# Loads of two chunks split over two queues, in longer runs, and a new order for the opening

## The chip, the cores and the metric

The kernel runs on one core of one Trainium2 chip. The metric is the device time of one execution in microseconds, lower is better. TensorE (PE) does the matrix products and the transposes into PSUM, VectorE (DVE), ScalarE (ACT) and GpSimd (POOL) do the elementwise work, and SyncE (SP) issues most of the transfers. Each engine works through its own list of instructions in the order in which they stand, and waits on semaphores for what other engines or transfers must have done.

## The reference

Attention over 4 batches, 8 heads, 768 tokens and head size 64, where a token sees the first 4 tokens (the sinks) and the last 128. Its output, seen as 3072 rows of 512, goes through a feed-forward layer that takes the largest of three products:

```python
scores = scale * np.matmul(q, k.transpose(0, 1, 3, 2))
is_sink = pos[None, :] < int(n_sink)
in_window = (rel >= 0) & (rel < int(window))
scores = np.where(is_sink | in_window, scores, -1000000000.0)
a = np.exp(scores - np.max(scores, axis=-1, keepdims=True))
a = a / (np.sum(a, axis=-1, keepdims=True) + 1e-09)
attn = np.matmul(a, v)
x = attn.transpose(0, 2, 1, 3).reshape(B * S, H * D)
h = np.maximum(np.maximum(x @ w1, x @ w2), x @ w3)      # 512 -> 768
out = h @ w_out                                         # 768 -> 512
```

All arrays are float32; the kernel computes in bf16 with float32 sums.

## The kernel before, in words

The 3072 rows are cut into 12 chunks of 256 tokens, three to a batch. The 8 heads are handled as 4 pairs. A chunk goes through these steps:

- `load` (L76 to L93): K, Q and V of the chunk, 512 KB each, from SyncE's queue. Partition p holds tokens 2p and 2p+1 of all heads, so a contiguous run is 2 tokens of one head, 512 bytes. A `gate` is a tiny POOL instruction that writes into the target first; the load waits for it, and so starts only when POOL has come that far (`pool_gate`, a memset) or when a weight has landed (`after`).
- `cast_qk` (L95) and `cast_v` (L104): float32 to bf16, in halves of four heads (`g` is 0 or 1) or quarters, each on an engine that the order names.
- `turn2` (L129, chunks 0 and 1) and `turn` (L109, chunks 2 and 3): four transposes on TensorE for a half, and one copy out of PSUM (the evacuation, L144 for K, L141 for Q), on the engine that the order names. With `turn2` K and Q of one half share a PSUM bank. From chunk 4 on, `turn_dma` does this by a transfer.
- `premask` (L251) puts the additive mask into PSUM with two matmuls on a pair ahead of its scores; pairs without it get a multiplicative mask after the exponential (`mask`, L289, on VectorE).
- `score` (L259), `expo` (L282, ScalarE), for chunks 1 and 2 of a batch also `sink_score` (L294); `sink_k` and `sink_v` (L226, L310) cut out the sinks' keys and values, `sink_init` (L216) prepares them.
- `av_open` and `av` (L324, L339): the product with V for a pair, then on VectorE a reciprocal (L355) and a product (L358) that normalise it.
- `xpose` (L364): eight transposes of the chunk's attention output, two evacuations.
- `ffn_h` (L383): a block of 8 matmuls (L390) for one third of the 768 columns and one of the three weights; ScalarE copies the first weight's result (L397), VectorE takes the largest with the other two (L401). `ffn_y` (L406) is the last product, `store` writes it.

PSUM has 8 banks, handed out in turn by `bank` and `give`. The weights come by GpSimd's queue (`load_w`, L236, in pieces of columns; `load_wo`, L244), which casts them on the way.

For chunks 0 to 3 the order is written out by hand, call by call (L454 to L655): it sets the order of the instructions on every engine and queue. `warm(n)` puts n idle matmuls into TensorE's list. After that a loop (L656) treats every chunk alike.

What the change touches: `load`, `cast_qk`, `turn2`, the first exponential (L168, which loads ScalarE's table) and the list from L454 on.

Of the kernel before, what the change touches and what calls it, by code (L numbers as in the profile page):

```python
# [16 lines left out]
def kernel(  # L17
# [13 lines left out]
    nc = tc.nc  # L31
# [17 lines left out]
    with tc.manual_schedule():  # L49
# [26 lines left out]
        def load(ci, what="kqv", gate=None, part=None, parts=1):  # L76
# [4 lines left out]
            for w in what:  # L81
# [13 lines left out]
        def cast_qk(ci, w, g, eng):  # L95

            if (ci, w) not in bfs:
                bfs[ci, w] = raw.tile([128, NP, 2, 2, D], BF16, tag=w + "_bf", name=w + "_bf")
            x, y = bfs[ci, w], raws[ci, w]
            f = eng.copy if eng is nc.scalar else eng.tensor_copy  # L100
            f(x[:, 2 * g:2 * g + 2].rearrange("q p i a d -> q p a i d"),  # L101
              y[:, 4 * g:4 * g + 4].rearrange("q (p a) i d -> q p a i d", a=2))
# [26 lines left out]
        def turn2(ci, w, g, eng=None):  # L129
# [10 lines left out]
            if w == "q":  # L140
                f(  # L141
                    qT[ci % RING][:, 2 * g:2 * g + 2].rearrange("q p i n r -> q (p i) (n r)"), pt)
            else:
                f(  # L144
                    kT[ci % RING][:, :, 2 * g:2 * g + 2].rearrange("q n p i r -> q n (p i) r"),
                    pt.rearrange("q x (n r) -> q n x r", r=64))
# [21 lines left out]
        nc.scalar.activation(one, wz[:, 0:1], AF.Exp)  # L168
        for x in vb:
            nc.vector.memset(x[:, :, :, D:D + 1], 1.0)  # L170

# [282 lines left out]
        warm(6)  # L454
        load(0, 'k')
        load(0, 'q', gate=pool_gate)
        warm(6)
        masks()
        premask(0, (2,))
        load(0, 'v', gate=pool_gate)  # L460
        cast_qk(0, 'k', 0, nc.gpsimd)
        sink_init()
        cast_qk(0, 'k', 1, nc.vector)
        premask(0, (3,))
        cast_qk(0, 'q', 0, nc.scalar)
        cast_qk(0, 'q', 1, nc.vector)
        turn2(0, 'k', 0, nc.scalar)
        load(1, 'k')
        premask(0, (0,))
        turn2(0, 'k', 1, nc.scalar)  # L470
        turn2(0, 'q', 1, nc.scalar)
        turn2(0, 'q', 0, nc.vector)
        score(0, (0,))
        expo(0, 0)
        load(1, 'q')
        premask(0, (1,))
        sink_k(0)
        cast_v(0, 1, 1, nc.vector)
        load_w(0, 0, 768)
        score(0, (1,))  # L480
        score(0, (2,))
        warm(3)
        cast_qk(1, 'k', 0, nc.vector)
        cast_v(0, 0, 0, nc.vector)
        cast_v(0, 1, 0, nc.gpsimd)
        expo(0, 2)
        expo(0, 1)
        load(1, 'v')
        av_open(0)
        load_w(1, 512, 768)  # L490
        score(0, (3,))
        cast_v(0, 0, 1, nc.vector)
        cast_qk(1, 'q', 1, nc.gpsimd)
        cast_qk(1, 'k', 1, nc.vector)
        av(0, 0)
        expo(0, 3)
        cast_qk(1, 'q', 0, nc.vector)
        turn2(1, 'k', 0, nc.vector)
        load_w(1, 0, 512)
        cast_v(1, 0, 1, nc.gpsimd)  # L500
        sink_v(0)
        av(0, 1)
        turn2(1, 'k', 1, nc.scalar)
        turn2(1, 'q', 0, nc.vector)
        turn2(1, 'q', 1, nc.vector)
        av(0, 2)
# [3 lines left out]
        av(0, 3)  # L510
        load_w(2, 0, 256)
        score(1, (0,))
        cast_v(1, 1, 1, nc.vector)
        score(1, (2,))
        premask(1, (3,))
        load_w(2, 256, 512)
        load(2, 'q', gate=pool_gate)
        score(1, (3,))
        load_w(2, 512, 768)
        expo(1, 0)  # L520
        xpose(0, 0, nc.vector)
        cast_qk(2, 'k', 1, nc.gpsimd)
        xpose(0, 1, nc.vector)
        expo(1, 2)
        sink_score(1)
        expo(1, 3)
        premask(1, (1,))
        load(2, 'v', gate=after(1))
        mask(1, 0)
        load_wo()  # L530
        cast_v(1, 1, 0, nc.vector)
        av_open(1)
        score(1, (1,))
        mask(1, 2)
        load(3, 'q', gate=after(0))
        ffn_h(0, 0, 0)
        cast_v(2, 1, 0, nc.gpsimd)
        expo(1, 1)
        av(1, 0)
        av(1, 2)  # L540
        ffn_h(0, 1, 0)
        av(1, 3)
        ffn_h(0, 2, 0)
        av(1, 1)
        ffn_h(0, 2, 1)
        xpose(1, 0, nc.scalar)
        xpose(1, 1, nc.vector)
        ffn_h(0, 0, 1)
        ffn_h(1, 0, 0)
        ffn_h(0, 1, 1)  # L550
        cast_qk(2, 'q', 0, nc.vector)
        ffn_h(1, 1, 0)
        ffn_h(1, 1, 1)
        cast_qk(2, 'k', 0, nc.scalar)
        cast_qk(2, 'q', 1, nc.scalar)
        turn(2, 'k', 1, nc.scalar)
        ffn_h(1, 2, 0)
        load(3, 'k', gate=after(1))
        turn(2, 'k', 0, nc.vector)
        ffn_h(1, 2, 1)  # L560
        ffn_h(1, 0, 1)
        turn(2, 'q', 0, nc.scalar)
        turn(2, 'q', 1, nc.scalar)
        ffn_h(0, 0, 2)
        score(2, (0,))
        score(2, (1,))
        ffn_h(1, 1, 2)
        expo(2, 0)
        ffn_h(0, 1, 2)
        score(2, (3,))  # L570
        expo(2, 1)
        cast_v(2, 0, 1, nc.vector)
        mask(2, 0)
        load(4, 'q', gate=pool_gate)
        score(2, (2,))
        load(3, 'v', gate=after(2))
        sink_score(2)
        mask(2, 1)
        ffn_h(0, 2, 2)
        ffn_h(1, 0, 2)  # L580
        expo(2, 3)
        cast_v(2, 1, 1, nc.gpsimd)
        expo(2, 2)
        cast_qk(3, 'q', 1, nc.vector)
        ffn_y(0, 0)
        load(4, 'k', gate=after(2))
        cast_v(2, 0, 0, nc.gpsimd)
        mask(2, 2)
        av_open(2)
        av(2, 0)  # L590
        cast_qk(3, 'q', 0, nc.gpsimd)
        cast_qk(3, 'k', 1, nc.scalar)
        mask(2, 3)
        av(2, 1)
        cast_qk(3, 'k', 0, nc.gpsimd)
        turn(3, 'q', 1, nc.vector)
        ffn_h(1, 2, 2)
# [152 lines left out]
```

## Time and profile before

| | |
|---|---|
| median of 3 runs | 179.97 us (179.81 to 180.43) |
| profiled execution | 180.04 us, its span 178.3 us |
| TensorE's granted clock | 1.000 |
| busy: PE, DVE, ACT, POOL | 170.4, 129.2, 81.4, 64.6 us |
| first warm-up matmul, first score, first FFN matmul (L390) | 1.20, 9.62, 18.33 us |
| Q of chunk 0: issued, cast begins | 1.38, 6.72 us |
| loads of 512 KB by SyncE, median from issue to landing | K 5.0, Q 6.1, V 7.1 us |

The span runs from the first to the last instruction of the profiled execution; the time of a run lies 1.7 us above it. In lines of the timeline the first number is the start in us, the second the busy time, then engine, line, operation, output and input, shapes and count; in brackets stands the idle time before it and what ended it. In lines of groups the numbers behind the bar are busy us, mean ns of one, and idle time of the engine before them. A line of a stretch gives the stretch, its length, the busy us of PE, PE's weight loads, DVE, ACT and POOL with counts, the granted clock, the transfer engines' busy share and GB/s.

### The profile page before, as it was taken

What the parts mean: (1) busy time and instruction counts of PE and PEld (TensorE: products, weight loads), DVE (VectorE), ACT (ScalarE), POOL (GpSimd) and SP (SyncE); (2) the same over time, 40 slices, a digit from 0 to 9 for tenths busy, and PEclk for the clock granted to TensorE, in tenths of its full rate; (3) what the DMA queues carried; (4) which work ended last, traced back from release to release, by engine and by line L of the source; (5) the groups of instructions that cost most, each with busy time, mean ns of one, the idle gap of its engine ahead of it and who ended that gap; (6) DMA issues with size and microseconds to landing.
All of it is one profiled execution on the core that took longest, in us unless ns stands there. A gap on an engine that the chain in (4) does not pass through costs nothing.

```text
span 178.3 us, 4662 instructions
## 1 busy us (share of the span) xinstructions
PE 170.4 (96%) x1873; PEld 126.3 (71%) x1873; DVE 129.2 (72%) x277; ACT 81.4 (46%) x163; POOL 64.6 (36%) x121
## 2 busy tenths in 40 slices
PE   7689999999999999999999999999999999999991
PEld 2445889766687587587696696696795795796870
DVE  3189752799799796696794994994975975976451
ACT  3386734863962922912715715615426426420210
POOL 4478620323663793282280670670550000000000
PEclk9999999999999999999999999999999999999999
DMA  5999999999999997995996996996978707202203
GB/s 147 290 286 209 243 212 249 214 288 290 332 184 258 295 170 184 256 279 129 293 282 136 299 210 152 296 215 155 285 211 136 162 0 64 119 6 56 118 0 118
DMA packets 69029, 34.90 MB, mean 196 GB/s; under 512 B 26512, under 2 KB 67472, under 8 KB 69008
## 3 DMA queue, kind: packets, MB, share of 16 engines
q1 hardware_dynamic: 64912, 31.33, 78.1%
q0 software_dynamic: 3952, 3.15, 11.3%
q8 instruction: 14, 0.23, 0.5%
q10 hardware_dynamic: 144, 0.13, 0.2%
q14 instruction: 7, 0.06, 0.1%
HBM read 25.17 MB, written 6.29 MB: 176 GB/s over the span
## 4 chain that ended last, share of the span: by engine, by line
PE 79%; DMA 13%; POOL 2%; ACT 2%; issue 1%; DVE 1%; POOLq 0%; ACTq 0%
PE h_ps L390 47%; PE y_ps L411 18%; DMA q_raw<-in_q_dram 9%; PE o L350 6%; PE st L274 5%; DMA w<-in_moe_w_dram 5%; PE o L332 1%; POOL w L239 1%; PE y_ps L421 1%; ACT q_bf L101 1%; PE sk L300 1%; PE xt L371 1%; ACT kT L144 1%; PE pt L115 1%; DVE h_sb L401 0%
## 5 line engine op out<-in xcount | busy, mean ns | idle before, releaser
L390 PE MATMUL h_ps<-xT,w 128*128 128x256 bf16 x864 | 103.8, 273 | 0.2 <-DVE h_sb L401 0.2
L390 PEld LDWEIGHTS <-w 128*128 128x128 bf16 x864 | 81.3, 98 | 11.7 <-issue 0.6
L401 DVE TENSOR_TENSOR h_sb<-h_sb,h_ps 128x512 bf16<-128x512 bf16 (+1 forms) x74 | 49.1, 669 | 17.5 <-PE h_ps L390 14.9
L397 ACT CAST h_sb<-h_ps 128x512 bf16<-128x512 f32 x36 | 21.1, 587 | 59.5 <-PE h_ps L390 59.4
L286 ACT ACTIVATE e_sb<-st 128x512 bf16<-128x512 f32 (+1 forms) x96 | 45.7, 573 | 5.1 <-PE st L274 5.0
L411 PE MATMUL y_ps<-wo,h_sb 128*128 128x512 bf16 x138 | 33.6, 380 | 0.0
L105 POOL CAST vb<-v_raw 64x512 bf16<-64x512 f32 x40 | 25.9, 648 | 19.8 <-DMA v_raw<-in_v_dram 18.2
L292 DVE TENSOR_TENSOR e_sb<-e_sb,msk 128x1024 bf16<-128x1024 bf16 (+1 forms) x42 | 30.0, 748 | 1.1 <-ACT e_sb L286 1.0
L101 POOL CAST k_bf<-k_raw 128x512 bf16<-128x512 f32 x17 | 12.8, 772 | 41.4 <-DMA k_raw<-in_k_dram 39.9
L413 DVE COPY y_sb<-y_ps 128x512 f32<-128x512 f32 x19 | 13.1, 691 | 13.0 <-PE y_ps L411 12.7
L411 PEld LDWEIGHTS <-h_sb 128*128 128x128 bf16 x138 | 11.9, 98 | 14.0 <-issue 2.5
L358 DVE TENSOR_TENSOR x_sb<-o,rc 128x256 bf16<-128x256 f32 x48 | 20.4, 424 | 1.7
L350 PE MATMUL o<-vb,e_sb 128*128 128x65 bf16 x352 | 18.3, 194 | 0.3 <-DVE vb L105 0.2
L350 PEld LDWEIGHTS <-e_sb 128*128 128x128 bf16 x352 | 16.0, 98 | 2.6 <-DVE vb L105 0.4
L274 PE MATMUL st<-qT,kT 64*128 64x128 bf16 (+1 forms) x256 | 14.3, 238 | 0.6 <-DVE qT L141 0.6
L274 PEld LDWEIGHTS <-kT 64*128 64x128 bf16 x256 | 8.2, 94 | 7.9 <-issue 6.2
L101 POOL CAST q_bf<-q_raw 128x512 bf16<-128x512 f32 x17 | 12.3, 742 | 4.1 <-DMA q_raw<-in_q_dram 3.7
L355 DVE RECIPROCAL rc<-o 128x4 f32<-128x4 f32 x48 | 8.4, 175 | 1.2 <-PE o L350 0.9
L306 ACT ACTIVATE e_sink<-sk 128x256 bf16<-128x256 f32 x8 | 3.1, 384 | 8.9 <-PE sk L300 8.9
L177 PE MATMUL warm<-wz 128*128 128x512 bf16 x15 | 5.2, 507 | 1.2 <-DVE wz L166 1.2
L101 DVE CAST q_bf<-q_raw 128x512 bf16<-128x512 f32 x5 | 2.1, 422 | 4.5 <-DMA q_raw<-in_q_dram 4.5
L239 POOL DMA_DIRECT2D w<-in_moe_w_dram x6 | 4.9, 810 | 0.1
(70 smaller groups left out, 69.8 us busy)
## 6 DMA issues: line engine op xcount, KB each, us to landing
k_raw<-in_k_dram SPq DMA_DIRECT2D x12, 512.0 KB, 5.0
q_raw<-in_q_dram SPq DMA_DIRECT2D x12, 512.0 KB, 6.1
v_raw<-in_v_dram SPq DMA_DIRECT2D x12, 512.0 KB, 7.1
out_dram<-y_sb SPq DMA_DIRECT2D x11, 512.0 KB, 3.7
w<-in_moe_w_dram POOLq DMA_DIRECT2D x4, 256.0 KB, 9.1
w<-in_moe_w_dram POOLq DMA_DIRECT2D x1, 768.0 KB, 8.3
wo<-in_moe_w_out_dram POOLq DMA_DIRECT2D x1, 768.0 KB, 10.7
w<-in_moe_w_dram POOLq DMA_DIRECT2D x1, 512.0 KB, 9.4
```

The source lines that it names most:

```text
L101: f(x[:, 2 * g:2 * g + 2].rearrange("q p i a d -> q p a i d"), y[:, 4 * g:4 * g + 4].rearrange("q (p a) i d -> q p a i d", a=2))
L105: eng.tensor_copy(vb[ci % RING][64 * i:64 * i + 64, n, :, 0:D], raws[ci, "v"][64 * n:64 * n + 64, :, i])
L274: nc.tensor.matmul(st[a][:, s:s + q1 - q0].rearrange("q n (i r) -> q n i r", i=2), lhsT=x[hp, n, p].rearrange("q i r -> q (i r)"), rhs=qc[ ...
L286: nc.scalar.activation(e[:, a, lo:], st[a][:, lo:], AF.Exp, scale=scale)
L292: (eng or nc.vector).tensor_mul(e[:, :, lo:], e[:, :, lo:], msk0 if lo else msk)
L350: nc.tensor.matmul(o[:, t, a], lhsT=e[:, a, s], rhs=vb[cv % RING][:, n, 2 * p + a], start=first, stop=True, skip_group_check=True)
L358: nc.vector.tensor_mul(xs[ci][:, :, p], o[:, :, :, 0:D], rc.unsqueeze(3).to_broadcast([128, 2, 2, D]))
L390: nc.tensor.matmul(hp[:, f].rearrange("q (i t r) -> q i t r", i=2, t=2), lhsT=w_sb[wi][:, ds, c0:c0 + 128], rhs=xTs[ci][:, :, ds].rearrang ...
L397: nc.scalar.copy(dst, hp)
L401: nc.vector.tensor_max(dst[:, x], dst[:, x], hp[:, x])
L411: nc.tensor.matmul(yp, lhsT=hs[ci][:, fb, t * 128:(t + 1) * 128], rhs=wo[:, fb], start=(fb == 0), stop=(fb == FB - 1))
L413: (nc.scalar.copy if eng is None else eng.tensor_copy)(ys[ci][:, t], yp)
```

## The change

The loads of chunks 0 and 1 are each cut into two, one issued by SyncE and one by ScalarE, without gates. For V each half holds four heads. For K and Q each half holds four heads on 64 partitions, and a partition holds four tokens of a head in one run of 1024 bytes. So the upper and the lower 64 partitions belong to different heads, and a token's place inside a transposed block is another: `cast_qk` regroups the heads, and the evacuations of `turn2` put the tokens back in order. They read PSUM with two neighbouring outputs 256 elements apart. K's evacuation becomes two copies of 256 elements in place of one of 512; a half `g` now covers pairs g and g+2.

The first exponential moves behind the first loads on ScalarE. The list for chunks 0 to 3 is ordered anew: which engine does a cast or an evacuation, the masks first, 16 warm-up matmuls in place of 15, one pair of chunk 1 with an additive mask in place of two, other gates and places for the loads of chunks 2 to 5 (Q of chunk 2 in two parts), other places for blocks of `ffn_h`. The loop is the same.

```diff
@@ load
+                if ci < 2:
+                    for g, e in enumerate((nc.sync, nc.scalar)):
+                        if w == "v":
+                            e.dma_start(
+                                out=dst[:, 4 * g:4 * g + 4],
+                                in_=src[b, 4 * g:4 * g + 4, t0:t0 + 256]
+                                    .rearrange("h (p i) d -> p h (i d)", i=2))
+                        else:
+                            e.dma_start(
+                                out=dst[64 * g:64 * g + 64].rearrange("r h i d -> r (h i d)")
+                                    .rearrange("r (h e) -> r h e", h=4),
+                                in_=src[b, 4 * g:4 * g + 4, t0:t0 + 256]
+                                    .rearrange("h (r j) d -> r h (j d)", j=4))
+                    continue
@@ cast_qk
+            if ci < 2:
+                n = H // 2
+                f(x[:, 2 * g:2 * g + 2].rearrange("q p i a d -> q (p i) a d")
+                  .rearrange("q j a d -> q a j d"),
+                  y[:, n * g:n * g + n].rearrange("q h i d -> q (h i d)")
+                  .rearrange("q (a j d) -> q a j d", a=2, d=D))
+                return
@@ turn2
             if w == "q":
-                f(
-                    qT[ci % RING][:, 2 * g:2 * g + 2].rearrange("q p i n r -> q (p i) (n r)"), pt)
+                f(qT[ci % RING][:, g:NP:2].rearrange("q h i n r -> q h i (n r)")
+                  .rearrange("q h i (m j) -> q h i m j", j=2),
+                  pt.rearrange("q (j i) (h m) -> q h i m j", i=2, h=2))
             else:
-                f(
-                    kT[ci % RING][:, :, 2 * g:2 * g + 2].rearrange("q n p i r -> q n (p i) r"),
-                    pt.rearrange("q x (n r) -> q n x r", r=64))
+                y = pt.rearrange("q x (h n m) -> q x h n m", h=2, n=2)
+                for n in range(2):
+                    f(kT[ci % RING][:, n, g:NP:2].rearrange("q h i (m j) -> q h i m j", j=2),
+                      y[:, :, :, n].rearrange("q (j i) h m -> q h i m j", i=2))
@@ the order, chunks 0 and 1 (after)
+        masks()
+        load(0, 'k')
+        load(0, 'q')
+        warm(9)
+        table()
+        load(0, 'v')
+        load(1, 'k')
+        cast_qk(0, 'k', 0, nc.gpsimd)
+        premask(0, (0,))
+        load(1, 'q')
+        load(1, 'v')
+        warm(2)
+        cast_qk(0, 'k', 1, nc.gpsimd)
+        cast_qk(0, 'q', 1, nc.vector)
+        turn2(0, 'k', 1, nc.vector)
+        cast_qk(0, 'q', 0, nc.scalar)
+        turn2(0, 'k', 0, nc.scalar)
+        turn2(0, 'q', 1, nc.scalar)
+        premask(0, (3,))
+        premask(0, (1,))
+        sink_init()
+        sink_k(0)
+        turn2(0, 'q', 0, nc.vector)
+        score(0, (0,))
...
+        warm(5)
...
+        load(2, 'q', part=0, parts=2, gate=pool_gate)
...
+        load(2, 'q', part=1, parts=2)
...
+        load(2, 'v')
...
+        ffn_h(1, 0, 0)
+        turn(2, 'q', 0, nc.scalar)
+        turn(2, 'k', 0, nc.vector)
...
```

More of the change, by code (lines that the diff above doesn't have):

```diff
@@ L472 @@
+        turn2(0, 'q', 1, nc.scalar)
+        premask(0, (3,))
+        premask(0, (1,))
+        sink_init()
+        sink_k(0)
         turn2(0, 'q', 0, nc.vector)
         score(0, (0,))
+        premask(0, (2,))
+        load_w(0, 0, 768)
+        score(0, (3,))
         expo(0, 0)
[L475 to L479, printed above, removed]
[L480 to L483 removed]
@@ L528 @@
[L528 to L536, printed above, removed]
+        expo(1, 0)
+        load(2, 'q', part=0, parts=2, gate=pool_gate)
+        score(1, (3,))
+        score(1, (1,))
+        load_w(2, 256, 512)
+        xpose(0, 0, nc.vector)
+        cast_v(1, 1, 1, nc.vector)
+        expo(1, 1)
+        load_w(2, 512, 768)
@@ L563 @@
-        turn(2, 'q', 1, nc.scalar)
-        ffn_h(0, 0, 2)
+        load(3, 'v', gate=pool_gate)
+        ffn_h(1, 1, 2)
+        expo(2, 1)
+        load(4, 'q', gate=after(0, 300))
+        ffn_h(0, 1, 2)
         score(2, (0,))
-        score(2, (1,))
-        ffn_h(1, 1, 2)
         expo(2, 0)
-        ffn_h(0, 1, 2)
+        mask(2, 1)
+        mask(2, 0)
         score(2, (3,))
[L571 to L574, printed above, removed]
+        cast_v(2, 0, 1, nc.gpsimd)
@@ L627 @@
         mask(3, 1)
-        score(3, (3,))
         mask(3, 0)
         expo(3, 2)
-        turn_dma(4, 'k')
-        cast_v(4, 0, 1, nc.gpsimd)
+        load(5, 'v', gate=after(2))
+        ffn_h(2, 0, 1)
         ffn_h(2, 0, 2)
         expo(3, 3)
-        cast_v(3, 1, 0, nc.gpsimd)
-        cast_v(4, 1, 1, nc.vector)
-        ffn_h(2, 0, 1)
+        av_open(3)
+        cast_v(4, 1, 1, nc.gpsimd)
+        mask(3, 2)
+        mask(3, 3)
         ffn_h(2, 2, 0)
-        mask(3, 3)
+        av(3, 0)
```

185 lines of the change are left out of this document (85 added, 100 removed).

## The prediction

> **What bounds the kernel now.** I read the page's shares first, then busy time by stretches, then the timeline of the opening, then mean durations by shape, and last the chain that ended last.
>
> ```profile
> PE 170.4 (96%) x1873; PEld 126.3 (71%) x1873; DVE 129.2 (72%) x277; ACT 81.4 (46%) x163; POOL 64.6 (36%) x121
> PE   7689999999999999999999999999999999999991
> ```
>
> PE is the bound. Only the first three slices (13 us) and the last one fall short, so the change can win only in the opening; what it does to the order of chunks 2 to 4 can hardly win, but it can lose. By stretches (busy us of each engine, granted clock, DMA share, GB/s):
>
> ```profile
> 2.00:4.00 2.00, 2.00 (x6) 0.73 (x5) 1.08 (x6) 0.23 (x2) 0.86 (x4) 1.00 0.89 245
> 4.00:6.00 2.00, 2.00 (x10) 0.93 (x9) 0.43 (x1) 0.00 (x0) 0.91 (x3) 1.00 1.21 298
> 6.00:8.00 2.00, 0.99 (x12) 0.72 (x10) 0.43 (x1) 1.22 (x3) 0.55 (x4) 1.00 1.21 290
> 8.00:10.00 2.00, 0.99 (x13) 0.75 (x13) 0.83 (x2) 0.98 (x3) 1.29 (x3) 1.00 1.21 291
> 14.00:16.00 2.00, 1.98 (x34) 1.26 (x31) 1.90 (x8) 0.84 (x3) 1.83 (x3) 1.00 1.17 213
> 16.00:18.00 2.00, 2.00 (x29) 0.97 (x28) 1.91 (x5) 2.00 (x5) 1.75 (x4) 1.00 1.32 202
> 45.50:46.00 0.50, 0.50 (x4) 0.19 (x2) 0.50 (x2) 0.50 (x2) 0.50 (x1) 1.00 1.10 395
> ```
>
> PE idles 2 us between 6 and 10, while the loads run at 290 GB/s. From 14 us PE is full; but VectorE is busy 1.90 of each 2 us there, so a longer VectorE operation in that stretch is not free.
>
> ```profile
> 1.38 5.31 DMA q_raw<-in_q_dram
> 20.14 10.03 DMA q_raw<-in_q_dram
> ```
>
> In the chain, Q of chunk 0 lands at 6.69. I count the opening from that instant.
>
> ```profile
> 6.72 0.43 DVE L101 CAST q_bf<-q_raw 128x512 bf16<-128x512 f32 x1 [1.38 <-DMA q_raw<-in_q_dram]
> 6.78 0.62 ACT L101 CAST q_bf<-q_raw 128x512 bf16<-128x512 f32 x1 [4.54 <-DMA q_raw<-in_q_dram]
> 7.30 1.07 ACT L144 COPY kT<-pt 128x512 bf16<-128x512 bf16 x2
> 8.42 0.61 PE L137 MATMUL pt<-ident,q_bf 128*128 128x128 bf16 x8 [1.43 <-ACT kT L144]
> 9.14 0.42 DVE L141 COPY qT<-pt 128x512 bf16<-128x512 bf16 x1 [1.99 <-PE pt L137]
> 9.62 0.34 PE L274 MATMUL st<-qT,kT 64*128 64x256 bf16 x4 [0.59 <-DVE qT L141]
> 9.97 3.29 ACT L286 ACTIVATE e_sb<-st 128x384 bf16<-128x384 f32 x8 [0.55 <-PE st L274]
> ```
>
> Q cast, both K evacuations on ScalarE, Q transposes, Q evacuation, first score: 2.93 us after the landing. The first FFN matmuls (L390) start at 18.33, which is 11.64 after the landing, and from there PE hardly waits. So the question is when the new kernel has done the same work. Durations by shape:
>
> ```profile
> L141 DVE COPY qT<-pt 128x512 bf16<-128x512 bf16 x3 | 1.2, 419 | 2.0 <-PE pt L137 2.0
> L423 DVE COPY y_sb<-y_ps 128x256 f32<-128x256 f32 x1 | 0.4, 425 | 0.6 <-PE y_ps L421 0.6
> L413 DVE COPY y_sb<-y_ps 128x512 f32<-128x512 f32 x19 | 13.1, 691 | 13.0 <-PE y_ps L411 12.7
> L144 ACT COPY kT<-pt 128x512 bf16<-128x512 bf16 x3 | 1.7, 585 | 0.3 <-PE pt L137 0.3
> L423 ACT COPY y_sb<-y_ps 128x256 f32<-128x256 f32 x1 | 0.4, 372 | 3.1 <-PE y_ps L421 3.1
> ```
>
> **The change, part by part.**
>
> *The loads.* K and Q of chunk 0 are 1.05 MB; summing the stretches they have moved by 5.85, and Q lands 0.85 later. With runs of 1 KB and two queues the rate is not in the trace. Best end: 395 GB/s (the stretch at 45.5, with runs of 4 KB) from 2.0 on, 2.66 us, landing at 5.5. Worst end: 220 GB/s, what the stretches from 24 to 28 show while two queues share the engines: 4.8 us, landing at 7.6. Between: the slow first microsecond (144 KB from 2 to 3) carries twice the bytes, then 350 to 395 GB/s, landing at 5.8 to 6.05. I take 5.9, since the nearest rows are those of whole loads without a rival; 0.8 earlier than now.
> [...]
>
> *ScalarE's six issues.* An issue takes 0.37 to 0.45 (the rows on SP and the one on ScalarE). Two go ahead of the table load, which ends near 3.2 instead of 2.2: hidden, ScalarE has nothing to do before Q lands. In the changed program's order the fifth and sixth issue of each queue wait for the K half and the Q half of chunk 0. On ScalarE the Q cast stands behind them, so it starts 0.35 after the landing. Ends: 0, if that half lands early; 1.7, if an issue is held as SP's fourth to sixth are now (1.38 and 1.74 each). I take 0.35: only half as many bytes stand in each queue.
>
> *Casts.* Same shapes (0.43 DVE, 0.62 ACT, 0.61 to 0.78 POOL). Both K casts of chunk 0 now run on POOL one after the other, done 1.5 after K lands (about 4.4), so by 5.9: hidden behind Q.
>
> *Evacuations.* The new layout reads PSUM with neighbours 256 elements apart, K in two copies of 256. No row shows such a read. On VectorE the rows go by words fetched: 512 neighbouring bf16 are 256 words, 0.42; 256 f32 words 0.425; 512 words 0.69. Ends: 0.29 for each K copy and 0.42 for Q if it still fetches pairs (the 128x130 copy took 0.29), 0.425 and 0.69 if each element is a fetch. I take the latter, as no two neighbours share a word: K 0.85 for 0.42, Q 0.69 for 0.42. ScalarE takes 0.59 for 512 of either type, so only K's split counts: 0.74 for 0.59.
> [...]
>
> *From Q's landing to the first score.* VectorE: cast 0.46, K evacuation 0.85 (now beside ScalarE, not behind its Q cast); PE: transposes 0.25, two masks' matmuls (L256) 0.65, transposes and hand-over 0.45; VectorE: Q evacuation 0.69. Sum 3.40 with the hand-overs (2.93 now); 2.9 with the cheap copies. ScalarE's own path (0.35+0.62+0.74) ends earlier, at 1.75.
>
> *From there to the first FFN matmul.* The fifth exponential frees the bank for sink_v: 0.35+5x0.41=2.40. Then VectorE's order is one chain: sink_v and hand-over 0.45, its copy 0.28, casts of K and Q of chunk 1 0.43 each, K evacuation 0.85, reciprocal and product of two pairs 1.2, Q evacuation 0.69, two pairs more 1.2. Then PE: eight transposes, sink scores, one pair's mask, one score, 1.4. Sum 9.33. The 16 warm-up matmuls (15 now), POOL's K cast of chunk 1 (ready near 11.7, when the chain needs it), its weight issues and the chunk-1 loads (landing before 12.1 even at today's rate) all lie beside that chain. On POOL the masks come first and sink_init after the K casts; sink_k follows the K evacuation, so w1's load is issued near 8.3 (9.08 now) and lands before 17.3, ahead of L390; were it late, PE would wait there by as much.
>
> *Sum.* 5.9+3.4+9.3=18.6; the sink part of chunk 1 (0.25), which now stands ahead of L390's first block, comes after it, so 18.9 against 18.33: +0.55. The pair-mask matmul saved in chunk 1 and the extra mask product (0.69 on VectorE, beside PE's FFN) are in it. The profiled execution took 180.04, 0.07 above the median of 179.97; against the median I forecast 180.5.
>
> *Chunks 2 to 4.* PE's idle time in the stretches from 14 to 60 sums to about 0.4, so at most that is won; I put the reorder at 0. Q of chunk 2 goes in two parts, one issue more on SP (0.37), which has nothing behind it but later loads; what could be late is its landing (third rival).
>
> **Rivals.**
> 1. *Faster: the strided evacuations cost what they cost now.* It is decided on VectorE between 6 and 16 us: two K evacuations at 0.58 and two of Q at 0.42 take 1.08 out of the sum, giving 17.8, -0.5; with the loads at 5.6, -0.8: 179.2. It is level with now when the four save 0.55 together. For it: 0.42 and 0.29 are rows of bf16 copies; against: the word count.
> 2. *Slower: the loads come no sooner.* Landing 6.7 with the strided copies: +1.35, 181.3. For it: DMA share is 1.2 already; against: 395 GB/s with long runs.
> 3. *Slower: Q of chunk 2 is late.* Its transposes move three FFN blocks forward (0.87 each), to about 27.5. Issued near 18.9, with today's 10.03 us it lands at 28.9, and cast and PE follow at 29.4: +1.9, 182.3. Against: 2 us of the opening's loads are gone by then, and it goes ahead of V; the row is of a time when w2 and wo ran beside it.
> 4. *Faster: the reorder removes waits.* -0.4 for all idle time that PE has there, and -0.8 if VectorE's chain runs without the hand-overs that I count between PE and VectorE: 179.3. For it: VectorE loses a K cast, a V cast and two evacuations to POOL and ScalarE in this stretch; against: what it loses is not on the chain.
>
> **How the numbers follow.** Forecast 0.45 (own range 180.1 to 181.1), rival 1 0.22, rival 2 0.13, rival 3 0.10, rival 4 0.10. 0.3% (0.54 us) is what a measurement of this kernel can tell from no change. The forecast lies on that edge: 0.21 of its chance is within, 0.24 above. Faster 0.31 (rivals 1 and 4, less 0.01), same 0.22, slower 0.47. Range 179.0 to 182.2: it takes in rivals 1, 2 and 4 and the loads' bounds for the most part, and leaves out the end of rival 3 and best loads with cheap copies.
>
> **What would show it.** Q of chunk 0 landing near 5.9, ScalarE's cast 0.35 behind VectorE's; VectorE's kT copies at 0.42 each and qT at 0.69; first score near 9.3; L390 from about 18.6 with PE waiting near 13 (K evacuation) and 16.5 (x of the last pair). Wrong if the copies take 0.3 and 0.42, if the landing is under 5.3, or if PE stalls at L390 or the chunk-2 transposes between 26 and 30.

## The result and the profile after

The changed kernel takes 185.42 us (median of 4 runs, 183.88 to 186.44), the kernel before 180.01 on the same chip: 1.028 times as long, 95% interval [1.0237, 1.0317]. Ratios here and below compare runs in the chip's faster state; medians and ranges hold all runs. Forecast were 180.5, and a range up to 182.2. The profiled execution of after is the run of 183.88, with a span of 182.1; that of before took 180.04, with a span of 178.3. So the traces show 3.84 us of the loss. The three other runs took 185.09 to 186.44, at mean granted clocks of 0.981 down to 0.972, where the profiled one has 0.990. If all that is missing is time at 0.50, the clock of the stretch from 12 to 14 us below, the profiled run spent about 3.5 us at it and the others 7 to 10 (an estimate from these means); that would account for most of the 1.5 us between the profiled run and the median, but there is no trace of those runs.

The page's busy shares and slices, after:

```profile
PE 170.6 (94%) x1859; PEld 126.9 (70%) x1872; DVE 129.6 (71%) x279; ACT 81.8 (45%) x166; POOL 62.5 (34%) x119
...
PE   7368899999999999999999999999999999999991
...
PEclk9978999999999999999999999999999999999999
```

TensorE is busy for as long as before (170.6 against 170.4 us) in a span that is 3.8 longer: the loss is mostly idle time, and it stands in the first four slices. There the granted clock also falls below full speed, which it did not before. By stretches (columns as before: busy us of PE, PE's weight loads, DVE, ACT, POOL; granted clock, DMA share, GB/s), after:

```profile
2.00:4.00 2.00, 2.00 (x6) 0.76 (x5) 1.08 (x6) 1.49 (x2) 0.73 (x3) 1.00 0.88 193
4.00:6.00 2.00, 1.69 (x7) 0.54 (x5) 0.00 (x0) 0.00 (x0) 0.00 (x0) 1.00 1.14 222
6.00:8.00 2.00, 0.62 (x8) 0.45 (x8) 0.00 (x0) 0.00 (x0) 1.83 (x7) 1.00 1.18 211
8.00:10.00 2.00, 0.37 (x5) 0.41 (x6) 1.09 (x3) 1.16 (x3) 0.18 (x2) 1.00 1.18 269
10.00:12.00 2.00, 1.15 (x13) 0.72 (x10) 0.98 (x2) 0.58 (x1) 1.71 (x5) 0.83 1.15 239
12.00:14.00 2.00, 2.00 (x18) 0.79 (x15) 0.92 (x2) 1.41 (x4) 1.96 (x5) 0.50 1.14 256
```

From 4 to 8 us the loads move 222 and 211 GB/s, where before moved 298 and 290, at a DMA share of 1.14 and 1.18 (1.21 before): the transfer engines are nearly as full as before and deliver a quarter less. (The share adds up the times of all packets, so it can pass 1.) From 6 to 10 us TensorE works 0.62 and 0.37 of each 2 us, and behind that comes the clock of 0.50.

The chain that ended last names the landing of chunk 0's Q (start, us, what):

```profile
1.54 6.84 DMA q_raw<-in_q_dram
```

It lands at 8.38, where before had 6.69. The timeline of the opening, after, from the cast of chunk 0's Q to the first FFN matmul (start us, us; the bracket is idle time and what ended it):

```profile
8.49 0.43 DVE L117 CAST q_bf<-q_raw 128x512 bf16<-128x512 f32 x1 [4.75 <-DMA q_raw<-in_q_dram]
8.82 0.62 ACT L117 CAST q_bf<-q_raw 128x512 bf16<-128x512 f32 x1 [5.18 <-DMA q_raw<-in_q_dram]
8.83 0.75 DVE L168 COPY kT<-pt 128x256 bf16<-128x256 bf16 x2
...
10.99 0.69 DVE L162 COPY qT<-pt 128x512 bf16<-128x512 bf16 x1 [1.42 <-PE pt L158]
11.74 0.51 PE L299 MATMUL st<-qT,kT 64*128 64x256 bf16 x4 [0.85 <-DVE qT L162]
12.93 1.14 PE L299 MATMUL st<-qT,kT 64*128 64x256 bf16 x12
...
21.89 1.05 PE L415 MATMUL h_ps<-xT,w 128*128 128x256 bf16 x8
```

VectorE's cast of Q starts at 8.49 (6.72 before), the first score at 11.74 (9.62 before), the first FFN matmul at 21.89 (18.33 before): 3.56 of the 3.84 us are lost by then.

### The profile page after: what moved, and what is told of

It is laid out like the page before. It is cut to its first block, busy times and chain, and to the rows that moved or that the text cites. A ratio compares the mean times of both kernels' runs of the same rounds, so it can differ in the third digit from the quotient of the medians.

```text
span 182.1 us, 4661 instructions
## 1 busy us (share of the span) xinstructions
PE 170.6 (94%) x1859; PEld 126.9 (70%) x1872; DVE 129.6 (71%) x279; ACT 81.8 (45%) x166; POOL 62.5 (34%) x119
## 4 chain that ended last, share of the span: by engine, by line
PE 86%; DVE 6%; DMA 4%; issue 2%; SPq 0%; DVEq 0%
PE h_ps L415 50%; PE y_ps L436 17%; PE st L299 6%; PE o L375 6%; DMA q_raw<-in_q_dram 4%; DVE h_sb L426 1%; PE o L357 1%; PE st L281 1%; PE pt L136 1%; DVE x_sb L383 1%; PE xt L396 1%; DVE qT L162 1%; PE warm L202 1%; DVE kT L168 1%; PE sk L325 1%
## 5 line engine op out<-in xcount | busy, mean ns | idle before, releaser
L436 PE MATMUL y_ps<-wo,h_sb 128*128 128x512 bf16 x126 | 32.7, 380 | 0.6
L122 POOL CAST k_bf<-k_raw 128x512 bf16<-128x512 f32 x16 | 10.9, 701 | 37.6 <-DMA k_raw<-in_k_dram 37.5
L375 PE MATMUL o<-vb,e_sb 128*128 128x65 bf16 x352 | 17.4, 193 | 0.0
L375 PEld LDWEIGHTS <-e_sb 128*128 128x128 bf16 x352 | 15.4, 98 | 1.6
L299 PE MATMUL st<-qT,kT 64*128 64x128 bf16 (+1 forms) x256 | 14.9, 245 | 1.4 <-DVE qT L162 1.1
L299 PEld LDWEIGHTS <-kT 64*128 64x128 bf16 x256 | 8.7, 96 | 8.4 <-issue 6.6
L122 POOL CAST q_bf<-q_raw 128x512 bf16<-128x512 f32 x14 | 10.2, 752 | 3.9 <-DMA q_raw<-in_q_dram 3.8
L202 PE MATMUL warm<-wz 128*128 128x512 bf16 x15 | 5.7, 523 | 1.4 <-DVE wz L189 1.2
L202 PEld LDWEIGHTS <-wz 128*128 128x128 bf16 x16 | 1.9, 127 | 4.2 <-issue 2.7
```

The source lines that it names most:

```text
L299: nc.tensor.matmul(st[a][:, s:s + q1 - q0].rearrange("q n (i r) -> q n i r", i=2), lhsT=x[hp, n, p].rearrange("q i r -> q (i r)"), rhs=qc[ ...
L375: nc.tensor.matmul(o[:, t, a], lhsT=e[:, a, s], rhs=vb[cv % RING][:, n, 2 * p + a], start=first, stop=True, skip_group_check=True)
L436: nc.tensor.matmul(yp, lhsT=hs[ci][:, fb, t * 128:(t + 1) * 128], rhs=wo[:, fb], start=(fb == 0), stop=(fb == FB - 1))
```

## The experiments

First the loads, then the clock, then the order, then the loads in the old order. In each diff the lines with a minus are those of the kernel that the text names.

**Two queues, but every transfer over all partitions.** The changed kernel, with K and Q of chunks 0 and 1 in halves by heads, like V; layout, casts and copies as before.

```diff
-                        if w == "v":
+                        if True:     # halves of 4 heads on 128 partitions
...
```

> The changed kernel, but K and Q of chunks 0 and 1 go as V does: each half is four heads on all 128 partitions in runs of two tokens, by both queues; casts and evacuations are the old ones. Theory R (rows: a half that writes only 64 partitions fills half of the memory's side and runs near 215 GB/s): the halves are whole again in partitions, so Q of chunk 0 lands near 6.7 as before the change; with the cheap evacuations the first FFN matmul follows 12.0 to 12.4 later, near 18.9, time near 181. Theory S (two queues at once slow each other, whatever the shape): Q still lands at 8.0 or later, first FFN matmul past 20, time 183 or more. Theory L (the long runs are slow): as theory R.

Measured: 181.44 (before beside it 180.19), ratio 1.0072 [1.0046, 1.0097]. Stretches of this run:

```profile
4.00:6.00 2.00, 2.00 (x7) 0.78 (x6) 0.00 (x0) 0.00 (x0) 1.26 (x3) 1.00 1.20 302
6.00:8.00 2.00, 1.15 (x15) 0.92 (x14) 0.76 (x2) 0.19 (x1) 0.59 (x4) 1.00 1.21 290
```

Two queues give the rate of one (298 and 290 before), and VectorE's Q cast starts at 6.83: two queues by themselves neither won nor lost bandwidth here. What this kernel loses in the opening shows on ScalarE:

```profile
6.83 0.37 ACTq L89 DMA_DIRECT2D q_raw<-in_q_dram  x1
6.83 0.43 DVE L115 CAST q_bf<-q_raw 128x512 bf16<-128x512 f32 x1 [3.10 <-DMA q_raw<-in_q_dram]
7.24 0.52 ACTq L89 DMA_DIRECT2D v_raw<-in_v_dram  x1
7.81 0.62 ACT L115 CAST q_bf<-q_raw 128x512 bf16<-128x512 f32 x1 [4.42 <-DMA q_raw<-in_q_dram]
```

The issues of chunk 1's Q and V stand ahead of ScalarE's cast and go out only when Q of chunk 0 lands, so the cast starts 0.98 behind VectorE's. The first score comes at 9.94 and the first FFN matmul at 19.21, where the order alone (below) has 9.46 and 18.41.

**One queue, but halves on 64 partitions.**

```diff
-                    for g, e in enumerate((nc.sync, nc.scalar)):
+                    for g, e in enumerate((nc.sync, nc.sync)):
```

> The changed kernel with both halves issued by SyncE, one after the other; layout, casts and evacuations as changed. Theory R (rows): still 215 GB/s, 1.05 MB take 4.9 us from 2 on, Q lands at 7.8 or later, time 183 or more. Theory S (two queues): one queue runs near 290 GB/s, Q lands by 6.9, first FFN matmul near 20, time near 182. Theory L (long runs): as R.

Measured: 185.49, ratio 1.0278 [1.0227, 1.0329], the same as the changed kernel. Its stretches:

```profile
4.00:6.00 2.00, 2.00 (x7) 0.70 (x5) 0.00 (x0) 0.00 (x0) 0.07 (x1) 1.00 1.14 209
6.00:8.00 2.00, 0.87 (x10) 0.45 (x8) 0.00 (x0) 0.00 (x0) 1.78 (x7) 1.00 1.19 215
```

Without a second queue the rate is as low: it belongs to the transfers on 64 partitions. From 4 to 6 us only K and Q move, here and in the changed kernel, and a packet of 1 KB takes 88 and 83 ns. From 6 to 8 about half of the bytes are V's. Its halves go over all partitions and are slow there too: a packet of 512 bytes takes 49 ns in the changed kernel, 34 in the kernel before. Why V suffers no run shows.

**Halves on every other partition.** Two queues and runs of 1 KB as in the changed kernel, but a half takes partitions g, g+2, and so on; the copies out of PSUM take the heads from the last index instead of the first.

```diff
-                                out=dst[64 * g:64 * g + 64].rearrange("r h i d -> r (h i d)")
+                                out=dst[g:128:2].rearrange("r h i d -> r (h i d)")
...
-                  pt.rearrange("q (j i) (h m) -> q h i m j", i=2, h=2))
+                  pt.rearrange("q (j i) (m h) -> q h i m j", i=2, h=2))
...
```

> The changed kernel with the halves on every other partition (even rows the first four heads, odd rows the others) in place of the lower and upper 64; two queues and runs of four tokens as changed, the same number of casts and evacuations. Theory R (rows): each half reaches all of the memory's side, Q lands between 5.5 and 6.5, the first FFN matmul 13.0 to 13.4 later, near 19.2, time near 181. Theories S and L: Q lands past 8, time 183.5 to 185.5 as changed.

Measured: 183.31 (181.46 to 184.38), ratio 1.0143 [1.0081, 1.0204]. The stretch that answers to the 222 of the changed kernel, and this kernel's waits of TensorE from 20 to 60 us (total, times, longest):

```profile
4.00:6.00 2.00, 1.89 (x7) 0.60 (x5) 0.00 (x0) 0.00 (x0) 0.82 (x2) 1.00 1.09 366
```

```profile
PE h_ps L415 <- DVE h_sb L426: 0.8, 1, 0.8
PE o L375 <- DVE e_sb L317: 0.6, 2, 0.4
```

The same bytes in the same runs by the same queues now move at 366 GB/s, 47 ns for a packet of 1 KB. VectorE's Q cast starts at 6.65, the granted clock stays 1.00, and the first FFN matmul comes at 19.59. The cast is hardly earlier than in the kernel before (6.72), since the stretch from 2 to 4 moves only 212 GB/s (245 before). And later TensorE waits 1.4 us for VectorE, where before has 0.2 and the changed kernel 0.3.

**Which 64 rows are slow.** Interleaving changes two things: rows no longer follow one another, and a transfer reaches all partitions. Three kernels with each half in two transfers of 128 KB separate them: even and odd rows inside a half, 32 adjacent rows, and every fourth row of all partitions (this one with the layout of the run before). The last two follow on the first, which did not decide.

```diff
+                            for z in range(2):
-                                out=dst[64 * g:64 * g + 64]        # changed kernel
+                                out=dst[64 * g + z:64 * g + 64:2]  # even/odd rows of a half
+                                out=dst[s0:s0 + 32]                # s0 = 64 * g + 32 * z
+                                out=dst[g + 2 * z:128:4]           # every fourth row
```

> As the changed kernel, with each K and Q half of chunks 0 and 1 in two transfers, the even and the odd rows of its 64 partitions (128 KB each): no transfer touches adjacent partitions, but each stays in one half of the partitions. Layout, casts and copies are those of the changed kernel. [...] Theory A (adjacent rows are what is slow, interleaving cures it): 300 GB/s and more once the issues are ahead, Q cast at 6.6 to 7.6, clock 1.00, first FFN matmul near 19.6, time 182.5 to 184. [...]

> The changed kernel with each K and Q half in two transfers of 32 adjacent rows (128 KB). Same number of transfers as in the run with even and odd rows inside a half. Theory P (reach over the partitions): 32 adjacent rows reach as far as 32 every-other rows of the same half, so K cast at 5.9 to 6.3 and 200 to 280 GB/s from 3 to 6, as there. Theory A (adjacency): slower than there, K cast after 6.4 and under 225 GB/s. A clock of 0.50 for a stretch between 8 and 18 in both.

> The kernel with interleaved rows (first score at 10.19, K cast at 5.18 there), each K and Q half in two transfers of 128 KB, every fourth row of all 128 partitions, so with as many issues as the run with even and odd rows inside a half (K cast there at 6.07, 239 to 280 GB/s from 3 to 6 us). Theory P (what counts is how far over the partitions a transfer reaches): K cast at 5.1 to 5.5, 300 GB/s and more from 3 to 6. Theory I (the doubled issues are the limit in that run): K cast at 5.9 to 6.2 and 240 to 280 GB/s again. In both, ScalarE's held issues put its cast of Q late, so the end is later than 183.3.

Measured: 187.47, ratio 1.0374 [1.0323, 1.0425]; 186.8, 1.0345 [1.0298, 1.0391]; 185.93, 1.0321 [1.0283, 1.0359]. The ends say little, since ScalarE's doubled issues hold up its cast of Q (to 12.37, 11.27 and 10.70). The loads say more. Stretches of the run with even and odd rows in a half:

```profile
3.00:6.00 3.00, 3.00 (x9) 1.10 (x8) 0.64 (x5) 1.49 (x2) 0.00 (x0) 1.00 0.93 262
10.00:11.00 1.00, 1.00 (x4) 0.16 (x2) 0.00 (x0) 0.00 (x0) 0.00 (x0) 0.50 1.15 249
```

of the run with 32 adjacent rows:

```profile
3.00:6.00 3.00, 3.00 (x9) 1.09 (x8) 0.65 (x5) 1.14 (x2) 1.13 (x3) 1.00 0.91 277
3.00:3.50 0.50, 0.50 (x3) 0.19 (x2) 0.43 (x4) 0.50 (x1) 0.00 (x0) 1.00 1.10 381
10.00:11.00 1.00, 0.00 (x0) 0.00 (x0) 0.00 (x0) 0.00 (x0) 0.00 (x0) 1.00 1.13 243
```

and of the run with every fourth row:

```profile
3.00:6.00 3.00, 3.00 (x10) 0.98 (x8) 0.64 (x5) 1.49 (x2) 0.47 (x1) 1.00 0.87 257
10.00:11.00 1.00, 1.00 (x4) 0.15 (x1) 0.00 (x0) 0.30 (x1) 0.00 (x0) 0.50 1.03 312
```

The lines from 3 to 6 us do not decide. The engines are not full there (a share of 0.87 to 0.93), and all three kernels move 257 to 277 GB/s whatever their rows. Theory I expects that of the doubled issues; that the issues are the cause is not shown.

The lines from 10 to 11 us do decide. By the packet records only K and Q of chunk 1 move there, and the engines are full (a share over 1) in all three kernels. The two whose transfers stay in one half of the partitions move 249 and 243 GB/s, with alternating or with adjacent rows, and the one whose transfers reach all partitions moves 312; a packet of 1 KB takes 74, 74 and 53 ns. So adjacency is out. With 32 adjacent rows the K cast even starts first, at 4.87, against 6.07 with alternating rows of a half and 5.53 with every fourth row (I had expected 5.9 to 6.3 and 5.1 to 5.5). Shorter issues may be the reason: the first four pairs took 0.87 to 0.94 us there and 1.28 to 1.63 with strided rows.

What counts is the reach, and not that of one transfer alone, but of all that move at the same time. The line from 3.0 to 3.5 us with 32 adjacent rows shows it: 381 GB/s, though every transfer stays in one half. In that half microsecond SyncE's queue started 105 packets of 1 KB, all into the lower half, and ScalarE's 81, all into the upper.

One more row of the trace belongs here. The changed kernel gives the lower half to one queue and the upper half to the other, so both halves could fill at once. The packet records show that they seldom do: in half-microsecond steps from 3.84 us on, SyncE's and ScalarE's queue started 110 and 8 packets of 1 KB, then 61 and 44, 7 and 101, 23 and 86, 87 and 17. The queues take turns in blocks, and during a block one half of the partitions is written. With 128-KB transfers the counts are closer to even (about 70 and 64, 75 and 58, 72 and 71 from 4 us on, with even and odd rows of a half).

Where only halves of K and Q move and the engines are full, in the stretches from 4 to 6 us, the rate is 222 GB/s with two queues and 209 with one. Why a half of the partitions is slower no run shows, nor the "half of the memory's side" of Theory R.

**The clock.** The changed kernel with 16 warm-up matmuls in the gap instead of 2.

```diff
-        warm(2)
+        warm(16)
```

> The changed kernel with 16 in place of 2 warm-up matmuls ahead of the first K transposes, so that TensorE does not sit idle from 5.7 to 7.3 and hardly from there to 9.6. The loads stay as they are (Q lands near 8.45). Theory C (the granted clock of 0.50 between 12 and 14 us comes from the idle time before it): the clock stays at 1.00, the first FFN matmul comes 0.7 to 1.5 earlier, near 20.8, and the time is 1 to 2 us under that of the changed kernel, with less spread between runs. Rival (the clock falls for another reason, or costs nothing because VectorE's chain sets the pace): first FFN matmul within 0.3 of 21.9, time as changed.

Measured: 183.99 (182.15 to 185.09), ratio 1.0235 [1.0192, 1.0278]. The scores of this run:

```profile
12.49 0.67 PE L299 MATMUL st<-qT,kT 64*128 64x256 bf16 x12
```

The loads are as late as ever (Q cast from 8.53, first score at 11.78), but the granted clock is 1.00 throughout, twelve score matmuls take 0.67 instead of 1.14, and the first FFN matmul comes at 20.97 instead of 21.89. So 0.92 us of the profiled loss up to there is the clock, a consequence of the idle time from 6 to 10 us. The span is 1.8 shorter than that of the changed kernel (180.3); the other 0.9 is idle time of TensorE between 20 and 100 us, which the changed kernel has (79.1 of 80 us busy) and this run has not (80.0), and no run shows why. The runs still spread (182.15 to 184.04, and one at 185.09) though the clock is 1.00 in all of them; what spreads them I have not found.

**The order alone.** The order of the changed kernel, with loads, casts and copies of before.

```diff
-                if ci < 2:
-                    for g, e in enumerate((nc.sync, nc.scalar)):
...
-                    continue
...
```

> The new order with the loads, casts and evacuations of the kernel before (whole loads of chunks 0 and 1 by SyncE in runs of two tokens, no gates there). Theory O (the new order itself costs about 1 us, which the run with halves on all partitions showed: first FFN matmul 12.4 after Q's landing in place of 11.6): Q lands near 6.5, first FFN matmul at 18.7 to 19.2, time 180.9 to 181.5. Rival (ScalarE's six issues cost it there): Q lands near 6.5, first FFN matmul by 18.3, time within 0.4 of the kernel before.

Measured: 181.47 (180.8 to 181.64, 10 runs); ratio 1.0037 [1.0006, 1.0067]. The opening keeps its time (first score 9.46, first FFN matmul 18.41), but TensorE waits for Q of chunk 2; timeline of this run:

```profile
29.36 0.43 DVE L101 CAST q_bf<-q_raw 128x512 bf16<-128x512 f32 x1 [3.00 <-DMA q_raw<-in_q_dram]
29.84 0.40 PE L115 MATMUL pt<-ident,q_bf 128*128 128x128 bf16 x4 [1.66 <-DVE q_bf L101]
```

That is my third rival. In the changed kernel it does not show, since TensorE arrives there late anyway. To test it, the transposes go behind two more FFN blocks:

```diff
-        turn(2, 'q', 0, nc.scalar)
-        turn(2, 'k', 0, nc.vector)
-        cast_qk(2, 'q', 1, nc.vector)
         ffn_h(0, 0, 2)
         ffn_h(1, 1, 1)
+        turn(2, 'q', 0, nc.scalar)
+        turn(2, 'k', 0, nc.vector)
+        cast_qk(2, 'q', 1, nc.vector)
+        ffn_h(1, 2, 1)
         turn(2, 'q', 1, nc.vector)
         score(2, (1,))
         turn(2, 'k', 1, nc.scalar)
-        ffn_h(1, 2, 1)
```

> The new order with whole loads, as in the run of the order alone, but chunk 2's transposes of Q and K stand behind two more FFN groups on TensorE (two times eight matmuls, 1.91 us for sixteen there). Theory (the 1.66 us idle before the transposes of chunk 2's Q is the only price of the new order once the opening is on time): the idle is gone or under 0.2 us, the span goes from 179.9 to about 178.2, and the time is about 179.5 to 179.9, no slower than before. Rival (the wait only passes on to the next thing that needs chunk 2, its scores, or another wait follows): a wait of over 1 us stays between 28 and 34 us, and the time stays at 180.8 to 181.5. First FFN matmul at 18.4 in both.

Measured: 180.52 (180.11 to 180.66, 12 runs), ratio 1.0015 [1.0001, 1.003]; the wait, in this run's list:

```profile
PE pt L115 <- DVE q_bf L101: 0.2, 1, 0.2
```

Of 1.7 us of wait 0.2 is left. The span is 178.7, 1.2 less than with the order alone. The rest comes back in small gaps: from 30 to 100 us TensorE is busy 69.1 of 70 us, and was 69.9. So the wait was the price of the new order, and without it the new order equals the old one; it does not beat it.

**Is the opening's chain worth shortening?** In this kernel, the group whose pair is scored first was put first:

```diff
-        turn2(0, 'k', 1, nc.vector)
+        turn2(0, 'k', 0, nc.vector)
         cast_qk(0, 'q', 0, nc.scalar)
-        turn2(0, 'k', 0, nc.scalar)
-        turn2(0, 'q', 1, nc.scalar)
+        turn2(0, 'k', 1, nc.scalar)
+        turn2(0, 'q', 0, nc.vector)
...
-        turn2(0, 'q', 0, nc.vector)
         score(0, (0,))
+        turn2(0, 'q', 1, nc.scalar)
```

> As the run with chunk 2's transposes later, and chunk 0's first group of pairs goes ahead of its second: its K is copied out by VectorE, its Q next, so that the first score needs no copy that stands behind the other group's. Expected first score 8.6 (9.46 with the order alone), 0.8 us sooner. Theory A (the opening's chain from the landing of Q0 sets the end): the first FFN matmul comes 0.4 to 0.8 sooner, the time falls to 179.0 to 179.4. Theory B (behind the first score the loads of chunk 1 set the pace, Q1 lands at 12 and V1 at 14 whatever chunk 0 does): first FFN matmul still at 18.2 to 18.4, time equal to the run beside it within 0.2.

Measured: 180.49 (12 runs), ratio 1.0017 [1.0004, 1.0031], the same as the run beside it. Two rows of its timeline on PE:

```profile
8.72 0.34 PE L276 MATMUL st<-qT,kT 64*128 64x256 bf16 x4
...
18.46 1.05 PE L392 MATMUL h_ps<-xT,w 128*128 128x256 bf16 x8
```

The first score comes 0.83 sooner (9.55 beside it), the first FFN matmul not at all (18.40 beside it). Theory B by its outcome, but the pace need not be the loads: GpSimd works without a gap from 8.10, when K's copies are done, through the sinks' copy, three weight issues (0.91, 0.74, 0.74) and three casts to the cast of chunk 1's Q at 12.90. So one cast was taken off it: K of chunk 1 goes by VectorE alone, casts and copies, ahead of the copy of the sinks' values.

```diff
         cast_v(0, 0, 1, nc.vector)
+        cast_qk(1, 'k', 0, nc.vector)
+        cast_qk(1, 'k', 1, nc.vector)
         expo(0, 1)
-        cast_qk(1, 'k', 0, nc.gpsimd)
+        turn2(1, 'k', 0, nc.vector)
+        turn2(1, 'k', 1, nc.vector)
...
         sink_v(0)
-        cast_qk(1, 'k', 1, nc.vector)
...
-        turn2(1, 'k', 0, nc.vector)
         av(0, 0)
-        av(0, 2)
-        turn2(1, 'k', 1, nc.scalar)
...
+        av(0, 2)
...
```

> As the run with group 0 first, and chunk 1's K goes by VectorE alone, before it copies the sink's values: VectorE stood idle there for 2.55 us (9.85 to 12.40), while GpSimd worked without a gap from 7.96 on (copy of the sink's keys, three weight loads of 0.74 to 0.91, four casts of 0.61 to 0.79) up to its cast of chunk 1's Q at 12.90. Theory B1 (GpSimd's row of work is what sets chunk 1's pace, and it begins when chunk 0's K copies are done): K of chunk 1 cast at 10.3 to 11.3 instead of 11.6 to 13.2, GpSimd's cast of Q at 12.3, transposes of chunk 1's Q at 13.2 to 13.5 instead of 14.35, first FFN matmul at 17.4 to 17.9 instead of 18.46 and the time 179.4 to 180.1. Theory B2 (the landing of chunk 1's Q at 12.2 and of its V at 14.0, or the exponentials of chunk 0, set it): first FFN matmul 18.2 to 18.5 again and the time equal to 180.5 within 0.2. If the first FFN matmul comes sooner, the wait for chunk 2's Q, whose loads start when the first weights have landed, can return with as much (0.2 now).

Measured: 180.81 (179.64 to 182.25, 12 runs), ratio 1.0046 [1.0018, 1.0075]. The first FFN matmul comes at 18.15, 0.31 sooner: GpSimd's row had a part in the pace, but less than B1 said, since VectorE's cast of Q now stands at 13.31, behind the sink's copy. And the end gains nothing: TensorE is busy 19.48 of the 20 us from 40 to 60, where the run before had 19.72. So 0.31 us of the opening is won, and 0.24 given back there.

**The new loads in the old order.** The changed loads, casts and copies with the order of before, three times: on 64 adjacent partitions by two queues, on interleaved ones by two, and on interleaved ones by SyncE alone.

```diff
+                    for g, e in enumerate((nc.sync, nc.scalar)):   # first two
+                    for g, e in enumerate((nc.sync, nc.sync)):     # third
+                                out=dst[64 * g:64 * g + 64]        # first
+                                out=dst[g:128:2]                   # second and third
```

> The old order with the changed loads (halves on 64 partitions, both queues) and their casts and evacuations. Theory R: Q lands near 8.4 as in the changed kernel, first score 3.1 to 3.3 later, near 11.6, first FFN matmul 20.0 to 20.8, time 182 to 183.5; so the loads make 2 to 3 of the 5.4 us and the new order most of the rest. Rival (the new order makes most of it): time within 1 of the kernel before.

> The old order with the halves on every other partition, both queues, runs of four tokens. Theory R: Q lands at 6.6 or before, the loads of chunk 1 run near 350 GB/s; the K copies on ScalarE cost 0.15 more each, so the first score comes at 9.6 to 9.9, and the time is 179.9 to 180.8. Rival (ScalarE's issues, which stand between its K copies and exponentials here, hold it): first score past 10.2, time 181 or more.

> As the kernel with interleaved rows in the old order, but all halves issued by SyncE. If the long runs alone raise the rate: 340 to 370 GB/s from 4 us on, Q lands by 6.6, time 179.6 to 180.3, under that with both queues, as ScalarE issues nothing. If two queues are needed for it: 290 GB/s, Q lands at 6.7 to 7.0, time 180.2 to 181.

Measured: 188.68, ratio 1.0429 [1.0365, 1.0493]; 188.11, 1.0387 [1.0333, 1.0441]; 182.0 (181.21 to 183.99, 10 runs), 1.0079 [1.004, 1.0118]. The first two are slow for a reason of their own. In the old order ScalarE's issues for chunk 1 stand behind its work on chunk 0; timeline of the second, ScalarE's queue and cast:

```profile
8.37 0.62 ACT L117 CAST q_bf<-q_raw 128x512 bf16<-128x512 f32 x1 [6.13 <-DMA q_raw<-in_q_dram]
8.44 0.62 ACTq L94 DMA_DIRECT2D k_raw<-in_k_dram  x1
12.54 0.61 ACTq L94 DMA_DIRECT2D q_raw<-in_q_dram  x1
```

Half of chunk 1's Q is issued at 12.54, when in before all of it has landed. In the second kernel Q of chunk 0 is late too (expected by 6.6, its casts start at 8.37), though its halves reach all partitions: by the packet records SyncE's half of Q ended at 5.20, and ScalarE's only at 7.82, while SyncE's queue went on with V and with K of chunk 1. So reach alone does not bring an operand in early; later loads on the other queue can pass it. And the two-queue load needs the new order, and no pair of runs splits the change into two clean parts. The third avoids this: 333 and 341 GB/s from 6 to 10 us, where before has 290 and 291; but only 210 from 4 to 6, at a DMA share of 0.85:

```profile
4.00:6.00 2.00, 2.00 (x10) 0.89 (x9) 0.43 (x1) 0.00 (x0) 1.07 (x4) 1.00 0.85 210
6.00:8.00 2.00, 1.08 (x12) 0.80 (x11) 0.43 (x1) 0.71 (x2) 0.45 (x4) 1.00 1.11 333
```

A half takes 0.6 to 0.7 us to issue here, where a whole load took 0.37 to 0.45. But that does not explain the 210: by 4 us SyncE had issued all of K and Q of chunk 0 (1.05 MB), and 0.45 MB had moved. Why the engines are not full there stays open. From 6 to 8 most bytes are V's in runs of 512 bytes, so 333 GB/s is not a matter of long runs alone. The Q cast starts at 7.30 and the first FFN matmul at 21.12; the granted clock falls here too, to 0.50 from 12 to 14 us.

None of these kernels beats the kernel before.

## Why the prediction was wrong, point by point

Where the 3.56 us up to the first FFN matmul come from, by differences between runs, one profile of each: order alone 18.41 against 18.33, 0.08; strided copies and ScalarE's issues, with loads at full reach, 19.59 against 18.41, 1.18 (0.80 of it stands in the run at 19.21, which has no strided copies); the slow landing, 20.97 against 19.59, 1.38; the clock, 21.89 against 20.97, 0.92. The last 0.28 of the 3.84 come later. Against the forecast of 18.9 the first FFN matmul is 3.0 late: 2.5 of that is Q's landing, 0.6 the way from the first score on, whose sum has no term for the clock.

- **The loads: the failed step.** I put Q's landing at 5.9, between ends of 5.5 and 7.6; it was 8.38. I bounded the rate by rows of before, whose transfers go over all 128 partitions (and the fastest of them, at 395, was mostly a store), and took the fast end because the new runs are longer. Over all partitions the new runs did move 341 to 381 GB/s. But I read the halves as a matter of queues and run length, and never asked which partitions a transfer touches. The worst end, 220 GB/s, was nearly the right rate, by luck: its row is of two queues sharing the engines. I ended it at 7.6 since I let it carry only the bytes of K and Q from 2.0 on. But the stretch from 2 to 4 moved only 193, and ScalarE's half of V began to move at 6.39, while SyncE's half of Q ended at 7.50; Q landed 0.88 after that.
- **Queues and partitions.** Two queues brought no rate (302 and 290 GB/s with both over all partitions, 298 and 290 with one in the kernel before). Halves of the partitions cost a quarter (222 and 211), and no term of the sum had that.
- **ScalarE's issues.** The lag of its cast was 0.33, as taken (0.35). An issue was not 0.37 to 0.45 but 0.56 to 0.83, except for V of chunk 1 (0.37 and 0.38). That stayed hidden; where the order put issues ahead of work it did not, with a lag of 0.98.
- **Strided copies.** Right. The word count was my estimate from the rows of before; the traces show times of copies and not what is fetched:

```profile
L168 DVE COPY kT<-pt 128x256 bf16<-128x256 bf16 x4 | 1.5, 414 | 0.0
L162 DVE COPY qT<-pt 128x512 bf16<-128x512 bf16 x2 | 1.4, 686 | 1.4 <-PE pt L158 1.4
L168 ACT COPY kT<-pt 128x256 bf16<-128x256 bf16 x4 | 1.3, 372 | 1.1 <-PE pt L158 1.1
```

  Means of 414, 686 and 372 ns, against 425 and 691, and ScalarE's pair 0.74 as taken. The first rival falls.
- **Landing to first score.** 3.40 forecast, 3.36 measured. Right.
- **First score to first FFN matmul.** 9.33 and 0.25 for the sink part, measured 10.15, and 9.19 in the run with the clock held at 1.00. So as a row of work the term was 0.39 too long, and the clock made up more than that. That the clock would fall to 0.50 behind two stretches in which TensorE is busy 0.62 and 0.37 of 2 us was in no step: the profile of before shows 1.00 everywhere, with 1 us idle in each 2 from 6 to 10, and I did not ask what longer idling would do. Moreover, the opening has slack: 0.83 saved on the first score moved nothing further on. My chain counted it as one line from Q's landing; part of the pace is GpSimd's row of issues and casts.
- **Chunks 2 to 4 at nothing.** Wrong, but hidden in the changed kernel. With the opening on time the third rival is real: landing at 29.3 (28.9 forecast), 1.7 us of wait (1.9 forecast). I had it at 0.10, and what I set against it (fewer loads left in its way) did not bring it forward.
- **The second rival** (landing 6.7, strided copies, +1.35) is the interleaved run: Q cast from 6.65 and a first FFN matmul 1.26 late. Yet that run takes 183.31, not 181.3: VectorE is late once more between 40 and 60, where TensorE is busy 18.74 of the 20 us.

## What to carry to other kernels

Before splitting a load, look at which partitions each piece reaches and not only at the length of its runs: pieces of 256 KB, each inside one half of the partitions, moved 209 to 222 GB/s here, whichever queue sent them, and pieces over all partitions 290 (512-byte runs) to 366 (1 KB). Pieces of 128 KB inside the halves came to 381 in a half microsecond in which both halves were written at once. The late operand cost twice here, 1.38 us as the wait and 0.92 as the clock of 0.50 that came behind TensorE's idle time, so price both. And when a wait vanishes behind a larger one, as the wait for chunk 2's Q did, it is still there for whoever removes the larger one.

## What the runs showed that was not expected

- Transfers that stay in one half of the partitions: 209 and 222 GB/s in pieces of 256 KB at a full DMA share (1.14), 243 and 249 in pieces of 128 KB. Over all partitions: 290 to 302 with runs of 512 bytes, 341 to 381 with runs of 1 KB, 312 in pieces of 128 KB.
- Two queues with large transfers take turns in blocks (110 and 8 packets in half a microsecond), so that giving each queue its own half of the partitions did not make the halves fill together.
- An issue on SyncE or ScalarE took 0.37 to 0.45 us for a whole load of the kernel before and 0.60 to 0.83 for a half of K or Q in runs of 1 KB.
- After two stretches with TensorE 0.62 and 0.37 of 2 us busy, the granted clock was 0.83, 0.50 and 0.81 in the next three; the missing 0.17, 0.50 and 0.19 of 2 us each are 1.72, or 3.4 us at 0.50. In steps of half a microsecond it is 0.83 from 11.0, 0.50 from 11.5 to 14.5, 0.76 from 14.5 and 1.00 from 15.0.
- First-score and first-FFN times moved apart: 0.83 us sooner at the one moved the other by nothing.
